# Two-stage packed attention with a gated convolution: gates per channel block, normalisation per head group, the 1e-9 as a column of the sums, v of batch 1 ahead of w_out, and a new order

## The chip, the core and the metric

The kernel runs on one core of a Trainium2 chip. A core has five engines that run beside each other, each with its own list of instructions in a fixed order: TensorE (PE, matrix products into PSUM), VectorE (DVE), ScalarE (ACT), GpSimd (POOL) and SyncE (SP), which here only issues transfers between the chip's memory and the core's SBUF. An instruction waits on semaphores for what it needs, and everything behind it on its engine waits with it.

The metric is the device time of one execution in microseconds (us). The chance of "faster" and "slower" in the prediction means a change of more than 0.5%.

## What is computed

Eight batches of eight heads, 576 rows, head size 64, and 32 packed rows per head. The packed rows attend to k and v; then q attends to the packed result, which serves as keys and as values. The heads are joined to 512 channels, which are gated by a sigmoid of a causal convolution over five rows and projected.

```python
scale = 1.0 / np.sqrt(q.shape[-1])
def sm_attn(qq, kk, vv):
    s = scale * np.matmul(qq, kk.transpose(0, 1, 3, 2))
    s = s - np.max(s, axis=-1, keepdims=True)
    a = np.exp(s)
    a = a / (np.sum(a, axis=-1, keepdims=True) + 1e-09)
    return np.matmul(a, vv)
p_packed = sm_attn(p, k, v)
out = sm_attn(q, p_packed, p_packed)
...
for k in range(K):                      # K = 5, x: the heads joined
    gate_pre += conv_w[k][None, None, :] * xp[:, k:k + S, :]
gate = 1.0 / (1.0 + np.exp(-gate_pre))
val = x @ w_val
return (gate * val @ w_out).astype(np.float32)
```

The three weight arrays arrive as 64-bit numbers and are rebuilt as 32-bit ones on the core.

## The kernel before, in words

Everything goes batch by batch. One generator function per step yields after each piece of work, and one table, `ORDER`, says which generator moves next. A token such as `g3.2` moves the gate of batch 3 by two pieces. Since every engine keeps its instructions in the order in which they are made (`InOrder`), the table is the schedule of all five engines; what waits for what follows from the data.

The steps of batch b, with the names that the trace shows:

- `load_k`, `load_q`, `load_v` ("K", "Q", "V") fetch km, qm and vm in two halves each, and `load_weights` ("L") the words of the weights. All of these go through `fetch`: a fetch waits until the fetch three before it has landed (`AT_ONCE = 3`). `load_p` ("P") fetches p for two batches outside that rule, in four small transfers, and ACT scales it. vm has two buffers, km and qm two each.
- `attn_pack` ("a"): PE makes the scores s of p and k for two groups of four heads (in PSUM). For each group g, DVE takes the maximum nb and ACT the exponential a1, with its row sums into sm. DVE adds 1e-9 to both sums and inverts them. Then for each group PE transposes a1 (at), ACT copies that to a1t, PE multiplies with vm (pv), and ACT scales the result into ppd.
- `packed_turned` ("p") transposes ppd into ppT; `packed_values` ("w") multiplies it with w_val (wp) and splits it into a rounded part wph (ACT) and a remainder wpl (DVE).
- `attn_out` ("s"): scores of q and ppT; per group DVE transposes them to t, takes the maximum mx, POOL subtracts it, and ACT takes the exponential. A column of 1e-9 stands beside each row of t.
- `weighted` ("t"): for both groups in turn, DVE sums and inverts (rs), POOL multiplies t by it, DVE transposes to a (a2 in the code), ACT rounds that to a2h, and the remainder a2l is taken by POOL (batches 0 to 2) or DVE.
- `mixed` ("x"): for batches 0 to 2 (`WHOLE`) the convolution is folded into PE: POOL multiplies ppd with the taps (kx), PE makes x out of a and kx, and ACT takes a tanh into sig. For batches 3 to 7 PE makes x, ACT copies it to xp, and `gate` ("g") computes the convolution: per block c of 128 channels ACT multiplies with the first tap, DVE adds the other four (four steps sig<-xp,cw,sig, each on the result of the one before), and ACT takes the tanh.
- `value` ("v"): per block PE multiplies a with the packed values in twelve matmuls (val), DVE joins it with the gate (sig<-sig,val, here "the last step of a gate"), ACT rounds to gvh, and POOL takes the remainder gvl.
- `project` ("o"): chunks of 128 rows; each is twelve matmuls of gvh and gvl with w_out (woh, wol). ACT copies a chunk out (osb) and SP writes it. For the last batch five chunks are begun before the last channel block is there.

The large PSUM tiles (scores, at, x, wp, val) share three buffers.

In the old order the gate of one batch is a single generator, so its blocks come strictly one after the other; the same holds for the two groups of `weighted`.

Of the kernel before, what the change touches and what calls it, by code (L numbers as in the profile page):

```python
# [57 lines left out]
v0 t1 a3.2 P4 a3 w1 O0.2 Q2 O0 v0 w1.2 v0 q2 p2 O0.2 x1 a3 x1 O0 x1 a3.2 O0 t1 a3.2 x1 L0 t1 O0.2 V3 q2 a3 x1 P4 O0.2
v1 x1 O0 K4 v1 s2 O0 V4 a3 O0 k4 a3 O0 v1 K4 O0 k4 s2 K5 s2.2 v1 s2 o0 s2 o0 p3 k4 Q3 v1.3 t2 v1.2 K5 v1 Q3 v1.2 a4 q3
o0 t2 a4.2 s2 a4.2 w2 V4 o0 s2 v1 t2 o0 w2 k5 s2 p3 a4 x2 q3 o0 v1 o0 w2 t2 s3 t2 o0 P6 Q4 t2 a4 v1 t2 s3 P6 s3 t2  # L60
s3.2 t2 s3.2 k5 s3 o0.2 a4 s3 v1 x2.3 Q4 a4 K6 a4 k5 a4.2 x2 o0 q4 t2 a4 t3 x2 v2 q4 x2 t3 a5 t3 v2 t3 a4.2 o1 t3 o0
t3 k6 K6 a5 t3 V5 v2 a5.2 t3 x3 Q5 x3 a4 v2 a5 k6 x3.2 t3 k6 v2 o1 v2 p4 v2 x3.3 t3 V5 Q5 o1 g3 a5.2 g3 p4 a5 v2 g3 o1
# [39 lines left out]
def packed_attention_gated_conv(  # L102
# [272 lines left out]
    def attn_pack(b):  # L375
# [6 lines left out]
        for g in range(G):  # L382
            nb = tile_of("nb1", [P, 1], F32, f"nb1_{b}_{g}")
            dve.tensor_reduce(nb, s1s[g], axis=AX.XY, op=ALU.max, negate=True)
            yield
# [76 lines left out]
            yield  # L462

    def weighted(b):
        rs = tile_of("rs2", [P, G, NBLK], F32, f"rs2_{b}")
        a2 = st["a2", b] = tile_of("a2", [P, G, S], F32, f"a2_{b}")
        ah = st["ah", b] = tile_of("a2h", [P, G, S], F32R, f"a2h_{b}")
        al = st["al", b] = tile_of("a2l", [P, G, S], F32R, f"a2l_{b}")
        for g in range(G):
            t3, r3 = st["t2", b][:, g], rs[:, g]  # L470
            dve.tensor_reduce(r3, t3, axis=AX.X, op=ALU.add)
            dve.reciprocal(r3, r3)
            yield
            t3 = t3[:, :, :NP]
            pool.tensor_tensor(
                t3, t3, r3.unsqueeze(2).broadcast_to([P, NBLK, NP]), op=ALU.mult
            )
            yield
            dve.transpose(a2[:, g], t3)
            yield  # L480
            act.copy(ah[:, g], a2[:, g])
            yield
            (pool if b in ON_POOL["al"] else dve).tensor_tensor(
                al[:, g], a2[:, g], ah[:, g].bitcast(F32), op=ALU.subtract
            )
            yield

# [85 lines left out]
                if c % 2:  # L573
                    yield

    def gate(b):
        if b in WHOLE:
            return
        for c in range(NC):
            x = st["xp", b, c // 2][:, c % 2]  # L580
# [3 lines left out]
            for kk in range(1, NT):
                dve.scalar_tensor_tensor(
                    acc,
                    x[:, kk : kk + S],
                    cw[:, c, kk : kk + 1],
                    acc,
                    op0=ALU.mult,  # L590
                    op1=ALU.add,
                )
                yield
            act.activation(acc, acc, AF.Tanh, scale=0.5)
            yield
# [86 lines left out]
    streams = {  # L682
        "K": load_k, "V": load_v, "Q": load_q, "P": load_p, "L": load_weights,
        "C": conv_weights, "W": value_weights, "O": out_weights,
        "k": keys, "a": attn_pack, "q": queries, "p": packed_turned, "s": attn_out, "t": weighted,
        "w": packed_values, "x": mixed, "g": gate, "v": value, "o": project,
    }
# [47 lines left out]
```

## Time and profile before

| | us |
|---|---|
| median of three runs | 284.44 (283.52 to 285.25) |
| the profiled execution | 284.7 |
| its span, first to last instruction | 282.9 |

The profile comes from one execution. Its page and the answers about its trace give, for each engine, when it was busy and what ended each idle time before an instruction: "[1.42 <-ACT sig]" means that the engine stood idle for 1.42 us and that an ACT instruction writing sig let it go on. In the rows, out<-in are the tiles written and read, then shapes, and xN the number of instructions joined in one row. Tile names leave out the numbers of batch and buffer. PEld is the loading of matmul weights, which runs beside the matmuls. SPq rows are issues of transfers; their landing comes later. Busy times of PE overlap, because matmuls are pipelined: the distance between two starts is the pace.

### The profile page before, as it was taken

The numbers are of one execution on the slowest core, as the hardware profiler recorded it, in microseconds if no ns is written. First come the engines' busy times: TensorE is split into PE (matmuls) and PEld (weight loads), VectorE is DVE, ScalarE is ACT, GpSimd is POOL, SyncE is SP. The second block draws the span as 40 slices with busy tenths as digits, with TensorE's granted clock in tenths as the row PEclk, the third lists the DMA queues.
The fourth block names the chain that finished last, engine by engine and source line by source line (L and its number), as shares of the span: only waits on it lengthen the run. The fifth ranks groups of instructions, "written<-read, shape, count | busy, mean of one in ns | idle before, by whom it ended". The sixth has DMA issues, their size and how long they took to land.

```text
span 282.9 us, 8353 instructions
## 1 busy us (share of the span) xinstructions
PE 251.4 (89%) x3603; PEld 186.8 (66%) x3603; DVE 237.2 (84%) x313; ACT 164.5 (58%) x307; POOL 129.4 (46%) x118
## 2 busy tenths in 40 slices
PE   0366397999999999999999999999999899998984
PEld 0144254776786777786878687758876688687763
DVE  2978779799789997789999999999998989687720
ACT  6245564677934664864746765667747645743321
POOL 1633577667788572423466324243156423422220
PEclk9989879999999999999999999999999999999999
DMA  7999989599649758816552540116111112111014
GB/s 258 330 292 310 226 270 264 164 238 287 179 153 306 207 161 237 257 43 203 150 180 81 191 132 37 39 75 179 66 39 41 48 63 76 39 74 39 0 50 172
DMA packets 25858, 43.54 MB, mean 154 GB/s; under 512 B 5834, under 2 KB 11998, under 8 KB 25822
## 3 DMA queue, kind: packets, MB, share of 16 engines
q1 hardware_dynamic: 25822, 43.02, 49.5%
q8 instruction: 28, 0.46, 0.7%
q14 instruction: 8, 0.07, 0.1%
HBM read 33.57 MB, written 9.44 MB: 152 GB/s over the span
## 4 chain that ended last, share of the span: by engine, by line
PE 55%; DVE 23%; ACT 9%; DMA 5%; issue 3%; POOL 2%; SPq 2%; POOLq 1%; ACTq 0%; DVEq 0%
PE o L85 20%; DVE sig L85 16%; PE val L85 11%; PE s L85 7%; PE x L85 7%; PE pv L85 4%; DMA vm<-in_v_dram 3%; ACT sig L85 3%; PE at L85 3%; PE wp L85 2%; POOL t L85 2%; SPq L85 2%; DMA p<-in_p_dram 1%; ACT gvh L85 1%; ACT osb L85 1%
## 5 line engine op out<-in xcount | busy, mean ns | idle before, releaser
L85 DVE SCALAR_TENSOR_TENSOR sig<-xp,cw,sig 128x576 f32<-128x576 f32 x80 | 75.0, 937 | 6.1 <-ACT sig L85 4.6
L85 POOL TENSOR_TENSOR gvl<-sig,gvh 128x576 fp32r<-128x576 f32 x32 | 49.3, 1541 | 55.8 <-ACT gvh L85 55.8
L85 PE MATMUL o<-woh,gvh 128*128 128x512 f32 x144 | 59.1, 411 | 0.8 <-ACT osb L85 0.7
L85 PE MATMUL o<-woh,gvl 128*128 128x512 f32 x144 | 57.2, 398 | 1.2 <-POOL gvl L85 1.1
L85 PE MATMUL o<-wol,gvh 128*128 128x512 f32 x144 | 56.9, 395 | 0.0
L85 PE MATMUL val<-a2h,wph 128*128 128x288 f32 x128 | 39.1, 305 | 0.0
L85 PE MATMUL val<-a2h,wpl 128*128 128x288 f32 x128 | 38.0, 297 | 0.9 <-DVE wpl L85 0.9
L85 PE MATMUL val<-a2l,wph 128*128 128x288 f32 x128 | 37.6, 294 | 0.0
L85 POOL TENSOR_TENSOR t<-t,rs 128x576 f32<-128x576 f32 x16 | 20.0, 1252 | 34.7 <-DVE rs L85 34.7
L85 PEld LDWEIGHTS o<-woh,gvh 128*128 128x128 f32 x144 | 27.0, 188 | 12.6 <-ACT osb L85 2.7
L85 PEld LDWEIGHTS o<-woh,gvl 128*128 128x128 f32 x144 | 27.1, 188 | 8.8 <-POOL gvl L85 2.5
L85 ACT ACTIVATE osb<-o 128x512 f32<-128x512 f32 x34 | 20.4, 599 | 18.4 <-PE o L85 14.8
L85 ACT CAST gvh<-sig 128x576 fp32r<-128x576 f32 x32 | 21.5, 671 | 16.4 <-DVE sig L85 16.0
L85 PEld LDWEIGHTS o<-wol,gvh 128*128 128x128 f32 x144 | 27.1, 188 | 5.0
L85 DVE SCALAR_TENSOR_TENSOR sig<-sig,val 128x576 f32<-128x576 f32 x32 | 23.8, 743 | 7.8 <-ACT sig L85 3.6
L85 POOL TENSOR_TENSOR t<-t,mx 128x576 f32<-128x576 f32 x16 | 21.2, 1328 | 18.3 <-DVE mx L85 18.3
L85 PEld LDWEIGHTS val<-a2h,wph 128*128 128x128 f32 x128 | 24.0, 188 | 4.4 <-issue 1.8
L85 PE MATMUL s<-kT,pT 32*32 32x288 f32 x512 | 15.5, 461 | 11.7 <-DVE kT L85 11.7
L85 PEld LDWEIGHTS val<-a2h,wpl 128*128 128x128 f32 x128 | 24.0, 188 | 2.1 <-DVE wpl L85 1.2
L85 ACT ACTIVATE sig<-sig 128x576 f32<-128x576 f32 x20 | 13.7, 685 | 19.4 <-DVE sig L85 19.1
L85 PEld LDWEIGHTS val<-a2l,wph 128*128 128x128 f32 x128 | 24.1, 188 | 0.0
L85 PEld LDWEIGHTS pv<-vm,a1t 96*32 96x32 f32 x768 | 12.8, 117 | 15.1 <-ACT p L85 5.1
(81 smaller groups left out, 444.2 us busy)
## 6 DMA issues: line engine op xcount, KB each, us to landing
km<-in_k_dram SPq DMA_DIRECT2D x16, 576.0 KB, 5.3
vm<-in_v_dram SPq DMA_DIRECT2D x16, 576.0 KB, 6.1
qm<-in_q_dram SPq DMA_DIRECT2D x16, 576.0 KB, 6.1
out_dram<-osb SPq DMA_DIRECT2D x36, 256.0 KB, 2.0
wv_words<-in_moe_w_val_dram SPq DMA_DIRECT2D x4, 512.0 KB, 4.5
wo_words<-in_moe_w_out_dram SPq DMA_DIRECT2D x4, 512.0 KB, 5.6
p<-in_p_dram SPq DMA_DIRECT2D x16, 64.0 KB, 5.9
cw_words<-in_moe_conv_w_dram SPq DMA_DIRECT2D x1, 20.0 KB
```

The source lines that it names most:

```text
L85: made = getattr(self.engine, op)(*args, **kw)
```

## The change

Five things change together.

1. The row sums of the first attention go into a new constant tile `sums`, one pair per batch and group, whose second element was set to 1e-9 by POOL at the start. DVE no longer adds 1e-9, but sums each pair into sm.
2. `weighted` is split: group 0 stays "t", group 1 becomes a stream of its own, "u". The work of each is unchanged.
3. `gate` now takes n = 4b + c and makes one block only, so that the blocks of a batch (g12 to g31) can be taken in any order.
4. The first half of v of batch 1 is fetched ahead of w_out.
5. The table is a new one over the whole length.

```diff
-V0 a0.2 W0 a1 W0 a0 W0 C0 a1 W0 a0 W0 Q0.2 a0 L0 p0 a1 K2 p0 q0.2 a1 P2 s0 a1 C0.2 s0 C0 O0 s0 O0 s0 V1 s0.2 a1 s0 O0
+V0 a0.2 W0 C0 W0 C0 a1 a0 Q0 W0 Q0 V1 a0 L0 a1 a0 K2 a1 q0.2 C0 p0 P2 p0 a1 W0 s0 a1 W0 s0 O0.2 s0.2 C0 s0.3 a1.3 O0
...
+    sums = const.tile([P, B, G, 2], F32, name="sums")
+    pool.memset(sums, 1e-9)
...
-                accum_out=sm[:, g : g + 1],
+                accum_out=sums[:, b, g, :1],
             )
             yield
-        dve.tensor_scalar_add(sm, sm, 1e-9)
+        dve.tensor_reduce(sm, sums[:, b], axis=AX.X, op=ALU.add)
...
     def weighted(b):
-        for g in range(G):
-            t3, r3 = st["t2", b][:, g], rs[:, g]
+        yield from weighted_group(b, 0)
+
+    def weighted_second(b):
+        yield from weighted_group(b, 1)
...
-    def gate(b):
-        if b in WHOLE:
-            return
-        for c in range(NC):
-            x = st["xp", b, c // 2][:, c % 2]
+    def gate(n):
+        b, c = divmod(n, NC)
+        x = st["xp", b, c // 2][:, c % 2]
```

Where the order moves instructions is best seen in the engines' own lists. First the transfers that SP issues in the front, from the first half of q of batch 0 on (vm_1_0 is the first half of v of batch 1, wo0 the first part of w_out), before and then in the changed kernel:

```order
L85 DMA qm_0_0_322<-in_q_dram 128x2x576
L85 DMA qm_0_1_324<-in_q_dram 128x2x576
L85 DMA wo0_words_327<-in_moe_w_out_dram 128x1024
L85 DMA km_2_0_335<-in_k_dram 128x2x576
L85 DMA p_2_345<-in_p_dram 32x8x64 x4
L85 DMA vm_1_0_399<-in_v_dram 96x4x384
L85 DMA vm_1_1_445<-in_v_dram 96x4x384
```
```order
L87 DMA qm_0_0_319<-in_q_dram 128x2x576
L87 DMA qm_0_1_322<-in_q_dram 128x2x576
L87 DMA vm_1_0_324<-in_v_dram 96x4x384
L87 DMA wo0_words_327<-in_moe_w_out_dram 128x1024
L87 DMA km_2_0_332<-in_k_dram 128x2x576
L87 DMA p_2_345<-in_p_dram 32x8x64 x4
L87 DMA vm_1_1_506<-in_v_dram 96x4x384
```

The first half of v has moved ahead of w_out, k and p; the second half still stands behind p.

Next ACT in the same part of the program (t2_0 is t of batch 0, a1t_1_0 and a1t_1_1 the turned exponentials of batch 1, cwb the spread taps), before and in the changed kernel:

```order
L85 ACTIVATE t2_0_350<-t2_0_350 128x18x32
L85 COPY cwb_73<-spread_429 128x5x2x64
L85 ACTIVATE t2_0_350<-t2_0_350 128x18x32
L85 COPY a1t_1_0_408<-at_1_0_409 96x768
L85 ACTIVATE p_2_345<-p_2_345 128x512
L85 CAST a2h_0_425<-a2_0_424 128x576
L85 ACTIVATE ppd_1_407<-pv_1_0_454,sm1_1_254 128x64
L85 ACTIVATE ppd_1_407<-pv_1_0_454,sm1_1_254 128x2x64
L85 COPY a1t_1_1_487<-at_1_1_488 96x768
```
```order
L87 ACTIVATE t2_0_355<-t2_0_355 128x18x32
L87 COPY a1t_1_0_409<-at_1_0_410 96x768
L87 ACTIVATE t2_0_355<-t2_0_355 128x18x32
L87 COPY cwb_73<-spread_434 128x5x2x64
L87 ACTIVATE ppd_1_408<-pv_1_0_450,sm1_1_259 128x64
L87 ACTIVATE ppd_1_408<-pv_1_0_450,sm1_1_259 128x2x64
L87 ACTIVATE p_2_345<-p_2_345 128x512
L87 COPY a1t_1_1_478<-at_1_1_479 96x768
```

The copy a1t_1_0 has moved ahead of the second exponential and of the taps, and the rounding a2h behind the second copy.

Last the end of DVE's list, from wpl of batch 7 on (sig_7_2 is block 2 of the last batch), before and in the changed kernel:

```order
L85 TENSOR_TENSOR wpl_7_3491<-wp_7_3468,wph_7_3490 128x1024
L85 SCALAR_TENSOR_TENSOR sig_7_0_3522<-xp_7_0_3419,cw_70,sig_7_0_3522 128x576 x4
L85 SCALAR_TENSOR_TENSOR sig_7_0_3522<-sig_7_0_3522,val_7_0_3508 128x576
L85 SCALAR_TENSOR_TENSOR sig_7_1_3531<-xp_7_0_3419,cw_70,sig_7_1_3531 128x576 x4
L85 SCALAR_TENSOR_TENSOR sig_7_2_3586<-xp_7_1_3421,cw_70,sig_7_2_3586 128x576
L85 SCALAR_TENSOR_TENSOR sig_7_1_3531<-sig_7_1_3531,val_7_1_3560 128x576
L85 SCALAR_TENSOR_TENSOR sig_7_2_3586<-xp_7_1_3421,cw_70,sig_7_2_3586 128x576 x3
L85 SCALAR_TENSOR_TENSOR sig_7_2_3586<-sig_7_2_3586,val_7_2_3599 128x576
```
```order
L87 SCALAR_TENSOR_TENSOR sig_7_3_3540<-xp_7_1_3423,cw_70,sig_7_3_3540 128x576
L87 SCALAR_TENSOR_TENSOR sig_7_0_3511<-sig_7_0_3511,val_7_0_3514 128x576
L87 SCALAR_TENSOR_TENSOR sig_7_2_3536<-xp_7_1_3423,cw_70,sig_7_2_3536 128x576
L87 SCALAR_TENSOR_TENSOR sig_7_1_3528<-sig_7_1_3528,val_7_1_3570 128x576
L87 SCALAR_TENSOR_TENSOR sig_7_2_3536<-xp_7_1_3423,cw_70,sig_7_2_3536 128x576
L87 SCALAR_TENSOR_TENSOR sig_7_3_3540<-xp_7_1_3423,cw_70,sig_7_3_3540 128x576
L87 SCALAR_TENSOR_TENSOR sig_7_2_3536<-sig_7_2_3536,val_7_2_3602 128x576
L87 SCALAR_TENSOR_TENSOR sig_7_3_3540<-xp_7_1_3423,cw_70,sig_7_3_3540 128x576 x2
```

The second list begins ten steps behind wpl: before, block 0 was finished right behind its four steps; now steps of other blocks stand between a chain's fourth step and its last one. On PE the last val of batch 7 has moved ahead of the first two products of the last chunks.

More of the change, by code (lines that the diff above doesn't have):

```diff
@@ L58 @@
[L58 to L62, printed above, removed]
@@ new lines @@
+V5 a5 g12 x3 s4 Q5 o1 g13 g12 a5.2 s4 v2 g12 a5 g12 s4.2 g13 o1 a5.2 s4 a5 s4 v2.2 g14 o1 g13 w3 v2.2 q5 g14 a6 o1.2
+w3 t4 Q6 a6 a5 v2 o1 a6.2 w3 g15 a5 g13 t4 s4 a5 g15 o1 q5 o1 g15 v3 p5.2 a6 g14 s4.2 o1 g15 o1 u4 g14 o1 Q6 s5 t4 v3
+o2 g14 u4 g15 v3.2 k7 s5 q6 s5 g15 v3 V6 v3 s5 o2 g14 t4 x4 o2 v3.3 u4 o2 s5.2 v3.2 s5.2 x4 v3 u4 v3 x4.2 k7 V6 o2 s5
+x4.2 a6 t4 v3.2 x4 v3 o2.2 g17 u4 a6.2 w4 a6 g16 o2 t5 u5 w4 a6 g17 a6.2 o2 g17.2 o2 a6 g18 g16 o2 g17 g19 o2 g16 w4
+a6 g16.2 g18 u5 a6 v4 u5 g18 g16 v4 t5 a6 K7 g17 g19 o3 v4.3 g18 t5 v4.2 g18 o3 g19 t5 v4 g18 q6 p6 v4 o3 g19 v4 g19
@@ L74 @@
+u7 o5.2 g27 v6 g27 x7 o5 v6 g27 u7 x7 v6 x7.2 v6.3 o5 x7 o5 t7 w7 x7 t7 w7.2 o6 g28.2 v7 o5 g29.3 g28 o6 x7 g30.2 o6
+g31 g29 g28 o6 g29 g28 g30 g31 o6 g28 o6 v7 g30 v7.2 g29 v7.4 o6 g30.2 g31 v7 o6 v7.3 g31 v7 g31.2 v7.3 o7.2 o6 o7.17
+o6.3
 """
@@ L464, in weighted, with weighted_group @@
     def weighted(b):
[L465 to L468, printed above, removed]
-        for g in range(G):
-            t3, r3 = st["t2", b][:, g], rs[:, g]
[L471 to L486, printed above, removed]
+        st["rs", b] = tile_of("rs2", [P, G, NBLK], F32, f"rs2_{b}")
+        st["a2", b] = tile_of("a2", [P, G, S], F32, f"a2_{b}")
+        st["ah", b] = tile_of("a2h", [P, G, S], F32R, f"a2h_{b}")
+        st["al", b] = tile_of("a2l", [P, G, S], F32R, f"a2l_{b}")
+        yield from weighted_group(b, 0)
+    def weighted_second(b):
+        yield from weighted_group(b, 1)
+    def weighted_group(b, g):
+        rs, a2, ah, al = (st[nm, b] for nm in ("rs", "a2", "ah", "al"))
+        t3, r3 = st["t2", b][:, g], rs[:, g]
+        dve.tensor_reduce(r3, t3, axis=AX.X, op=ALU.add)
+        dve.reciprocal(r3, r3)
+        yield
+        t3 = t3[:, :, :NP]
+        pool.tensor_tensor(
+            t3, t3, r3.unsqueeze(2).broadcast_to([P, NBLK, NP]), op=ALU.mult
+        )
+        yield
+        dve.transpose(a2[:, g], t3)
+        yield
+        act.copy(ah[:, g], a2[:, g])
+        yield
+        (pool if b in ON_POOL["al"] else dve).tensor_tensor(
+            al[:, g], a2[:, g], ah[:, g].bitcast(F32), op=ALU.subtract
+        )
+        yield
     def packed_values(b):
@@ L574, in convolved @@
                     yield
-    def gate(b):
-        if b in WHOLE:
-            return
-        for c in range(NC):
-            x = st["xp", b, c // 2][:, c % 2]
-            acc = st["sig", b, c] = tile_of("sig", [P, S], F32, f"sig_{b}_{c}")
-            act.mul(acc, x[:, :S], cw[:, c, 0:1])
-            yield
[L584 to L595, printed above, removed]
+    def gate(n):
+        b, c = divmod(n, NC)
+        x = st["xp", b, c // 2][:, c % 2]
+        acc = st["sig", b, c] = tile_of("sig", [P, S], F32, f"sig_{b}_{c}")
+        act.mul(acc, x[:, :S], cw[:, c, 0:1])
+        yield
+        for kk in range(1, NT):
+            dve.scalar_tensor_tensor(
+                acc,
+                x[:, kk : kk + S],
+                cw[:, c, kk : kk + 1],
+                acc,
+                op0=ALU.mult,
+                op1=ALU.add,
+            )
+            yield
+        act.activation(acc, acc, AF.Tanh, scale=0.5)
+        yield
     def value(b):
@@ L684, in packed_attention_gated_conv @@
         "C": conv_weights, "W": value_weights, "O": out_weights,
[L685 removed]
+        "k": keys, "a": attn_pack, "q": queries, "p": packed_turned, "s": attn_out, "t": weighted, "u": weighted_second,
         "w": packed_values, "x": mixed, "g": gate, "v": value, "o": project,
```

27 lines of the change are left out of this document (13 added, 14 removed).

## The prediction

> **What bounds the kernel now.** First the page's totals.
>
> ```profile
> span 282.9 us, 8353 instructions
> PE 251.4 (89%) x3603; PEld 186.8 (66%) x3603; DVE 237.2 (84%) x313; ACT 164.5 (58%) x307; POOL 129.4 (46%) x118
> ```
>
> PE and DVE are both near the span. Shares over the whole hide where the rest lies, so I read the busy times by stretches next.
>
> ```profile
> 0.00:50.00 50.00, 26.58 (x644) 16.22 (x658) 37.27 (x55) 26.58 (x54) 25.95 (x28) 0.90 0.96 278
> 50.00:130.00 80.00, 78.93 (x1551) 59.19 (x1520) 70.01 (x95) 50.52 (x106) 48.69 (x44) 1.00 0.68 204
> 130.00:240.00 110.00, 108.66 (x1232) 83.05 (x1230) 105.56 (x138) 70.42 (x122) 44.87 (x40) 1.00 0.30 97
> ```
>
> The columns are PE, PEld, DVE, ACT, POOL, granted clock, DMA share and GB/s. Up to 50 us the DMA engines are 96% busy and PE stands still for 23.4 us. From 50 to 240 us PE idles for 1.07 + 1.34 = 2.4 us of 190. A busy PE need not be PE at its pace, so the rows of its timeline follow, at the one place in the middle where it visibly waits.
>
> ```profile
> 222.55 0.39 PE L85 MATMUL o<-woh,gvl 128*128 128x512 f32 x1
> 222.78 0.29 PE L85 MATMUL val<-a2h,wph 128*128 128x288 f32 x1
> 223.97 0.40 PE L85 MATMUL val<-a2h,wpl 128*128 128x288 f32 x1 [0.89 <-DVE wpl L85]
> ```
>
> An output matmul takes 0.39 us from start to end, but the next instruction starts 0.23 us after it: this is the pace to measure by. 36 output chunks of 12 matmuls at 0.23 us are 99 us, the largest part of PE's work, and the change leaves every matmul in place: **PE is at its pace**. The kernel can gain only where PE waits: in the first 50 us, at this wpl, and behind the last gates. DVE is the second bound: it has 9.99 us of idle time from 50 to 130 us, but only 4.44 us from 130 to 240. The chain of waits shows what held the front:
>
> ```profile
> 25.86 9.90 DMA vm<-in_v_dram
> ...
> 40.63 0.66 PE x L85 x12
> ...
> 46.58 1.47 issue
> 48.05 1.19 PE x L85 x21
> ```
>
> PE waits for v of batch 1 from 25.86 to 35.76 us (25.86 + 9.90), and the convolution x starts at 40.63. At 46.58 lies a gap that no wait explains. PE's own timeline has the wait at its matmul:
>
> ```profile
> 35.90 1.51 PE L85 MATMUL pv<-vm,a1t 96*32 96x64 f32 x48 [4.92 <-DMA vm<-in_v_dram]
> ```
>
> **The change: v of batch 1.** The DMA queue's rows say when it can come.
>
> ```profile
> 17.12 2.16 SPq L85 DMA_DIRECT2D qm<-in_q_dram  x2
> 22.11 0.35 SPq L85 DMA_DIRECT2D wo_words<-in_moe_w_out_dram  x1
> ```
> ```profile
> DMA to landing us min/median/max: 4.4/6.1/10.2
> ```
>
> At most three fetches are under way, so the fetch behind the two of q starts when v of batch 0, three fetches earlier, has landed, at 22.11. That slot passes from w_out to the first half of v. With the median landing v is there at 28.2 us, with the longest at 32.3. Nothing is saved in bytes: w_out, k and p of batch 2 each go one place back, and so does the second half of v behind them, which stays the later of the two.
>
> The wait of 4.9 us is not won whole, because another input of the same matmul is nearly as late: a1t, which ACT copies.
>
> ```profile
> 31.60 0.68 ACT L85 ACTIVATE t<-t 128x576 f32<-128x576 f32 x1 [1.89 <-POOL t L85]
> 32.19 0.67 ACT L85 COPY cwb<-spread 128x640 f32<-128x640 f32 x1
> 33.82 0.68 ACT L85 ACTIVATE t<-t 128x576 f32<-128x576 f32 x1 [0.95 <-POOL t L85]
> 34.41 0.78 ACT L85 COPY a1t<-at 96x768 f32<-96x768 f32 x1
> ```
>
> In the old order a1t ends at 35.19, and sooner v alone would be worth 0.7 us. In the new order this copy stands directly behind the first exponential: it starts at 32.19 and ends at 32.97, so pv can start at 33.1 instead of 35.90. That is 2.8 us. The new wait is a1t behind the first t of POOL.
>
> **The normalisation per pair.** Next on PE, after a transpose, the packed values and a second pv, is the convolution of batch 0 (x at 40.63). It needs kx and both transposed halves of a2, hence POOL:
>
> ```profile
> 30.41 1.16 POOL L85 TENSOR_TENSOR t<-t,mx 128x576 f32<-128x576 f32 x1 [4.13 <-DVE mx L85]
> 32.52 1.27 POOL L85 TENSOR_TENSOR t<-t,mx 128x576 f32<-128x576 f32 x1 [0.95 <-DVE mx L85]
> 33.98 1.41 POOL L85 TENSOR_TENSOR t<-t,rs 128x576 f32<-128x576 f32 x1 [0.20 <-DVE rs L85]
> 35.34 1.55 POOL L85 TENSOR_TENSOR kx<-ppd,cwb 128x640 f32<-128x640 f32 x1
> 36.98 1.41 POOL L85 TENSOR_TENSOR a2l<-a,a2h 128x576 fp32r<-128x576 f32 x1
> 38.35 1.34 POOL L85 TENSOR_TENSOR t<-t,rs 128x576 f32<-128x576 f32 x1
> ```
>
> The split lets the second t·rs stand right behind the first, with kx after it and both a2l later. DVE's second maximum also moves ahead of the sum and its reciprocal, 0.59 + 0.17 us by the rows below. So the second subtraction starts 0.76 sooner, at 31.76, and ends at 33.0, its exponential (0.68) 33.7, the row sum and reciprocal (about 1.0, the maximum over the same tile being 0.74) 34.8, the second t·rs (1.34) 36.2 and kx (1.55) 37.8: x starts at 37.9, 2.7 us sooner. What is late next is a2l for the first val, now behind three steps of w_out on POOL: 37.8 + 3 x 1.3 + 1.41 + 1.55 + 1.41 = 46.1 us; before it lie x, which now runs until 49.24 (48.05 + 1.19), and the scores of batch 2, so it is hidden as long as these come no more than 3 us sooner. ACT's product on p of batch 2 also stands ahead of the second a1t copy. I take 2.7 us, or 4.2 if the unexplained 1.47 us do not return, and between them **3.3**. The bounds are 0.7 (v alone) and 6.4 (the whole wait of 4.9 and the gap).
>
> **The 1e-9 as a column.** The addition becomes a sum over two elements.
>
> ```profile
> L85 DVE TENSOR_REDUCE mx<-t 128x18 f32<-128x576 f32 x16 | 11.9, 744 | 0.3
> L85 DVE TENSOR_SCALAR sm<-sm 128x2 f32<-128x2 f32 x8 | 4.7, 591 | 0.2 <-ACT a L85 0.2
> L85 DVE RECIPROCAL sm<-sm 128x2 f32<-128x2 f32 x8 | 1.3, 166 | 0.3
> ```
>
> The trace has no sum of this size. It lies between the reciprocal of the same tile (8 x 0.166 = 1.3 us) and the big sums (8 x 0.744 = 6.0): DVE gains 3.4 or loses 1.3. Two elements are nearest to the reciprocal, so 3.4 us less DVE work, of which I count 2.2 behind the front (five or six of the eight). PE is the bound, so I book nothing for it; it is cover.
>
> That row's mean of 591 for two elements is more than three times the reciprocal's 166. [...]
>
> **The gates per channel block, and the order.** No instruction is added; the same 20 chains of six operations interleave. The gain is at the end, where DVE waits for the tanh of the chain it has just finished, and PE for gvl:
>
> ```profile
> 257.16 0.82 DVE L85 SCALAR_TENSOR_TENSOR sig<-xp,cw,sig 128x576 f32<-128x576 f32 x1 [1.42 <-ACT sig L85]
> ...
> 262.86 0.76 DVE L85 SCALAR_TENSOR_TENSOR sig<-sig,val 128x576 f32<-128x576 f32 x1 [0.75 <-ACT sig L85]
> ```
> ```profile
> 260.39 0.39 PE L85 MATMUL o<-wol,gvh 128*128 128x512 f32 x1
> 261.55 0.50 PE L85 MATMUL o<-woh,gvl 128*128 128x512 f32 x1 [0.77 <-POOL gvl L85]
> ```
>
> Of the last batch's chains DVE loses 1.42 and 0.75 us here; in the new order other chains' steps stand in both places, so some 2.2 us go. PE loses 1.16 - 0.23 = 0.93 us at 261.55; the new order also puts its last val, twelve matmuls, ahead of these products, which covers that. At 223.97 PE lost 0.89 us to wpl, ahead of which DVE now has the same work less the shorter sums. Together **1.8 us**, bounds 0 (DVE comes no sooner than PE) and 1.8. Against them I set **0.7 us** of new waits: the middle has 2.4 us of PE idle time now, and a new order has others (bounds 0 and 2.4).
>
> Sum: 284.7 us (span 282.9 and 1.8 around it) - 3.3 - 1.8 + 0.7 = 280.3. The profiled run is 0.3 us over the median of 284.44; for the median that gives **280.0 us**, 1.6% less.
>
> **The rivals.** *Nothing is carried.* PE starts sooner, but DVE, which idles for only 4.4 us from 130 to 240, comes no sooner to the gates. Then the front's gain is waited away at val and o, and only the wpl wait and part of the end stay: 284.4 - 1 = 283.4. For it speaks DVE's 96% there; against it that its work ahead of each gate is not more, that PE outputs come sooner, and that 10 us of idle time lie before 130.
>
> *The loads come too late.* w_out, k and p of batch 2 land later, and ACT waits for p ahead of the a1t of batch 1. p is issued just ahead of 25.86 now and one fetch later then, about 2.2 us (the two of q took 2.16); by the longest landing above it is there at 28.1 + 10.2 = 38.3. The product, the copy (0.78 each at most) and the second pv then leave x at 40.6, where it is now: the same 283.4.
>
> *Slower: the interleaved gates meet POOL.* The price is in the group's row:
>
> ```profile
> L85 DVE SCALAR_TENSOR_TENSOR sig<-xp,cw,sig 128x576 f32<-128x576 f32 x80 | 75.0, 937 | 6.1 <-ACT sig L85 4.6
> 246.33 3.38 DVE L85 SCALAR_TENSOR_TENSOR sig<-xp,cw,sig 128x576 f32<-128x576 f32 x4 [0.19 <-ACT sig L85]
> 251.13 4.61 DVE L85 SCALAR_TENSOR_TENSOR sig<-xp,cw,sig 128x576 f32<-128x576 f32 x4
> 252.84 1.44 POOL L85 TENSOR_TENSOR gvl<-sig,gvh 128x576 fp32r<-128x576 f32 x1 [7.86 <-ACT gvh L85]
> ```
>
> A clean step takes 0.82 us (the end of one overlaps the next: 3.38 for four), so 80 would take 65.6; 9.4 us are lost. The chain at 251.13 is 1.2 us longer than the one at 246.33, and POOL works beside it. From 130 to 240 POOL is busy 41% of the time. If the interleaving doubles these losses, DVE has 9.4 us more; 1.1 us of its idle time is left after the front's gain, and 2.2 us come off with the sums: 280.0 + 6.1 = 286.1, and more if more steps meet. It is slower than before from 4.4 + 1.1 + 2.2 = 7.7 us more, six or seven such steps. [...]
>
> *More than forecast.* The gap at 46.58 goes and every gvl wait too: 284.4 - 4.2 - 1.8 = 278.4 without new waits, and 276.2 with the whole wait of 4.9 us besides the gap.
>
> **How the numbers follow.** My forecast 0.55, more than forecast 0.2, nothing carried or loads late 0.14, slower 0.11. The range leaves out a tenth on either side: 276.0 (front wait, gap and end all gone) to 286.0 (the gates' losses doubled). A measurement of this kernel tells 0.5%, 1.4 us, from no change: faster 0.75, same 0.14, slower 0.11.
>
> **What would show it.** In the changed profile: v of batch 1 issued near 22 us and landed by 29; its pv at about 33 after an ACT wait, x at about 38, the first k scores of batch 2 at 45 to 47 instead of after 49.2; sm sums near 0.17 us each; no ACT wait over 1 us on DVE after 240; the sig<-xp group at 75 us or less; PE without gaps from 50 us. I am wrong if p or the second v holds ACT or PE before 40 us, if PE shows new waits for DVE or POOL from 60 to 240 us, or if the sig group has grown.

## The result, and the profile after

| | before | changed |
|---|---|---|
| median, us | 284.44 (283.52 to 285.25) | 279.74 (279.26 to 280.44) |
| the profiled execution, us | 284.7 | 279.26 |
| its span, us | 282.9 | 277.5 |

The ratio of the times is 0.985 (95% interval 0.981 to 0.989). The forecast was 280.0. The time was right; where it came from was not, as the rows below show. First the totals of the changed kernel and its busy times by stretches (PE, PEld, DVE, ACT, POOL, granted clock, DMA share, GB/s):

```profile
span 277.5 us, 8356 instructions
PE 252.7 (91%) x3603; PEld 187.6 (68%) x3603; DVE 227.8 (82%) x313; ACT 164.1 (59%) x307; POOL 132.0 (48%) x119
```
```profile
0.00:50.00 50.00, 30.74 (x689) 17.77 (x689) 36.65 (x55) 27.43 (x56) 25.70 (x28) 0.90 0.93 279
50.00:130.00 80.00, 78.98 (x1518) 59.38 (x1500) 68.86 (x99) 51.06 (x105) 49.76 (x44) 1.00 0.70 203
130.00:240.00 110.00, 110.00 (x1245) 83.85 (x1243) 102.70 (x137) 70.64 (x125) 50.05 (x44) 1.00 0.31 98
```

PE has no idle time left from 130 to 240 us, and DVE has lost 9.4 us of work over the whole. The grouped rows of DVE say where: the gate steps (75.0 us before) and the sums (4.7 us before, as additions). In the rows stand busy time, mean of one in ns, and idle time before them.

```profile
L87 DVE SCALAR_TENSOR_TENSOR sig<-xp,cw,sig 128x576 f32<-128x576 f32 x80 | 66.1, 870 | 1.5 <-ACT sig L87 1.2
...
L87 DVE TENSOR_REDUCE sm<-sums 128x2 f32<-128x4 f32 x8 | 1.1, 142 | 0.2 <-ACT a L87 0.2
```

To see which stage gave the time, take two points on PE that have the same set of matmuls ahead of them in both kernels, whatever their order (689 and 3275): the first val, and the packed values wp of batch 6. PE's timeline, first of the kernel before, then of the changed one:

```profile
51.23 0.40 PE L85 MATMUL val<-a2h,wph 128*128 128x288 f32 x1
...
218.87 1.09 PE L85 MATMUL wp<-wv,ppT 64*32 64x512 f32 x16
```
```profile
50.26 0.40 PE L87 MATMUL val<-a2h,wph 128*128 128x288 f32 x1
...
217.17 1.09 PE L87 MATMUL wp<-wv,ppT 64*32 64x512 f32 x16
```

Up to the first val the changed kernel gains 51.23 - 50.26 = 0.97 us. From there to wp it takes 166.91 us instead of 167.64, 0.73 less. From wp to the end of the span it takes 60.31 instead of 64.06: **3.75 us of the 5.4 come from the last 64 us**. The prediction had put 3.3 into the front and 1.8 behind wp.

These two points and the end are the measure for all experiments below. The ratios compare fast executions, but the profiled one of f2 was a slow one (284.5 us), so of its three stretches only the last is used.

### The profile page after: what moved, and what is told of

It reads as the page before. It is cut to its first block, busy times and chain, and to the rows that moved or that the text cites. A ratio compares the mean times of both kernels' runs of the same rounds, so it can differ in the third digit from the quotient of the medians.

```text
span 277.5 us, 8356 instructions
## 1 busy us (share of the span) xinstructions
PE 252.7 (91%) x3603; PEld 187.6 (68%) x3603; DVE 227.8 (82%) x313; ACT 164.1 (59%) x307; POOL 132.0 (48%) x119
## 4 chain that ended last, share of the span: by engine, by line
PE 85%; DMA 8%; DVE 2%; ACT 1%; SPq 1%; issue 1%; POOL 0%; ACTq 0%
PE o L87 37%; PE val L87 19%; PE x L87 8%; PE s L87 8%; PE pv L87 5%; DMA km<-in_k_dram 4%; PE at L87 4%; PE wp L87 3%; DMA qm<-in_q_dram 3%; DMA wv_words<-in_moe_w_val_dram 2%; PE ppTt L87 1%; SPq L87 1%; DVE mx L87 1%; DVE t L87 1%; DVE qT L87 1%
## 5 line engine op out<-in xcount | busy, mean ns | idle before, releaser
L87 POOL TENSOR_TENSOR gvl<-sig,gvh 128x576 fp32r<-128x576 f32 x32 | 51.0, 1595 | 69.5 <-ACT gvh L87 69.4
L87 DVE SCALAR_TENSOR_TENSOR sig<-xp,cw,sig 128x576 f32<-128x576 f32 x80 | 66.1, 870 | 1.5 <-ACT sig L87 1.2
L87 PE MATMUL val<-a2h,wpl 128*128 128x288 f32 x128 | 37.9, 296 | 0.5 <-issue 0.5
L87 PE MATMUL s<-kT,pT 32*32 32x288 f32 x512 | 16.9, 479 | 11.9 <-DVE kT L87 11.6
L87 POOL TENSOR_TENSOR t<-t,rs 128x576 f32<-128x576 f32 x16 | 20.6, 1296 | 8.6 <-DVE rs L87 7.1
L87 PEld LDWEIGHTS pv<-vm,a1t 96*32 96x32 f32 x768 | 13.7, 123 | 13.4 <-issue 3.7
L87 DVE STREAM_TRANSPOSE qT<-qm 128x1152 f32<-128x1152 f32 x16 | 21.6, 1357 | 0.8 <-DMA qm<-in_q_dram 0.8
```

Source lines behind the costliest of these rows:

```text
L87: made = getattr(self.engine, op)(*args, **kw)
```

## The experiments

Times are medians. "To val", "to wp" and "to end" are the three stretches in us, from each run's profiled execution. The ratio is to runs of the kernel before on the same chip.

| run | time | ratio (95%) | to val | to wp | to end |
|---|---|---|---|---|---|
| before | 284.44 | 1 | 51.23 | 167.64 | 64.06 |
| changed | 279.74 | 0.985 (0.981-0.989) | 50.26 | 166.91 | 60.31 |
| e1_cw_sooner | 280.56 | 0.990 (0.986-0.993) | 51.71 | 166.83 | 60.32 |
| e2_cw_wo | 280.33 | 0.988 (0.983-0.992) | 49.77 | 166.78 | 60.32 |
| e3_v_late | 279.94 | 0.985 (0.981-0.990) | 50.09 | 166.51 | 60.32 |
| e4_before_v_sooner | 284.51 | 1.004 (1.001-1.006) | 50.22 | 167.79 | 64.07 |
| e5_before_sums | 284.55 | 1.002 (1.000-1.005) | 52.69 | 166.56 | 64.10 |
| e6_after_scalar | 282.26 | 0.995 (0.992-0.998) | 50.08 | 168.75 | 60.91 |
| e7_last_serial | 284.64 | 1.003 (1.000-1.006) | 48.77 | 167.85 | 65.14 |
| e8_all_serial | 314.75 | 1.108 (1.104-1.113) | 51.25 | 189.75 | 71.42 |
| f1_front_of_after | 285.77 | 1.005 (1.002-1.008) | 52.39 | 169.15 | 64.06 |
| f2_tail_of_before | 283.08 | 0.994 (0.991-0.998) | 51.08 | 168.95 | 62.69 |
| f3_busy_pe | 280.42 | 0.988 (0.984-0.992) | 50.38 | 168.96 | 60.34 |
| f4_busy_pe_cw_wo | 280.29 | 0.986 (0.981-0.990) | 51.64 | 166.37 | 60.33 |

The last column repeats to 0.1 us wherever the order behind wp is the same (e6 apart, of which more below). The first varies by 3.6 us between changed, e7 and f1 (50.26, 48.77, 52.39), whose order on PE is the same up to there: a single front says little. The medians say more: they lie 4.70 us apart, 3.75 of that is behind wp, and so less than 1 us is left for everything ahead of it.

### What held the front: the copy of cw

The forecast had the first pv of batch 1 at 33.1 us, behind its a1t copy. It starts at 36.06, 1.5 us after that copy has ended. PE and DVE of the changed kernel:

```profile
36.06 1.51 PE L87 MATMUL pv<-vm,a1t 96*32 96x64 f32 x48 [3.17 <-ACT cwb L87]
```
```profile
33.61 1.34 DVE L87 TENSOR_SCALAR wo_words<-wo_words 128x512 uint32<-128x512 uint32 x1
...
35.84 0.12 DVE L87 COPY cw<-cwps 128x20 f32<-128x20 f32 x1
```

The row names ACT's cwb, with which pv shares nothing. But pv goes into the PSUM tile "mid", of which there is one, and cwps sits in it until DVE has copied cw, at 35.96.

```diff
-s0 O0.2 s0.2 C0 s0.3 a1.3 O0 s0 t0 C0 s0 C0 | C0 u0 t0
+s0 O0.2 s0.2 C0 s0.3 C0 a1.3 O0 s0 t0 s0 C0 | C0 u0 t0        # e1
+s0 O0.2 s0.2 C0 s0.3 C0 a1.3 s0 t0 s0 C0 | C0 u0 O0 t0        # e2
```

e1_cw_sooner:

> The changed kernel, with DVE's copy of the transposed taps (cw<-cwps) 5 places sooner on DVE, behind the first maximum instead of behind the first row sum. Theory 1: the first pv of batch 1 waits at 36.06 us because cwps holds the only PSUM buffer called mid until that copy ends at 35.96. Then pv starts behind its own a1t copy, at 34.6 to 34.8, x some 1.1 to 1.4 us sooner than 41.64 (kx, which ends at 40.48, is next), and the time is 278.4 to 279.0 us. Rival: pv waits for ACT's cwb, as its row names it. Then pv stays at 36.0 and the time at 279.7.

e2_cw_wo:

> As the run before, and in addition the first word step of w_out on DVE (1.34 us at 33.61) behind the two row sums instead of ahead of them. Theory 1: the row sums start at 34.0 instead of 34.87, both t times rs and kx come 1 us sooner, x is held only by PE's own chain from pv (34.7 + 5.6 = 40.3 us), and the time is 278.2 to 278.6. Rival (cwb): 279.3 to 279.7, since pv stays at 36.0 and x with it.

PE of e1 and of e2:

```profile
35.48 1.51 PE L87 MATMUL pv<-vm,a1t 96*32 96x64 f32 x48 [0.79 <-ACT a1t L87]
```
```profile
34.20 1.51 PE L87 MATMUL pv<-vm,a1t 96*32 96x64 f32 x48 [1.85 <-ACT a1t L87]
```

In both runs pv now starts 0.05 us after a1t has ended (35.43 and 34.15 on ACT) and names it: the theory of the PSUM tile holds, and the releaser printed in the changed kernel was wrong. But neither run is faster. In e2 pv is 1.86 us sooner and x 1.85 (39.79 instead of 41.64), but only twelve of its products are done before 41.72; the first val is 0.5 us sooner, and the median is not below 279.74. In the profile of e1 the granted clock stayed at 0.50 from 28.1 to 45.1 us, and the first 80 products of x took 4.49 us instead of 2.78, which hides the sooner pv there. So a sooner pv of batch 1 does not by itself bring the front's end sooner.

### Sooner v by itself

e3_v_late puts the first half of v back behind p of batch 2 in the changed order; e4_before_v_sooner does this one edit in the old order.

```diff
-Q0 W0 Q0 V1 a0 L0 a1 a0 K2 a1 q0.2 C0 p0 P2 p0
+Q0 W0 Q0 a0 L0 a1 a0 K2 a1 q0.2 C0 p0 P2 V1 p0                # e3
-Q0.2 a0 L0 p0 ... O0 s0 V1 s0.2
+Q0.2 V1 a0 L0 p0 ... O0 s0 s0.2                               # e4
```

> The changed kernel with the first half of v of batch 1 fetched where it was before, behind p of batch 2. If the sooner fetch is what the front gained by, pv of batch 1 starts at 38 or later (v lands one fetch later than in the old order) and the time is 281 or more. If the copy of cw holds that pv anyway, v lands at about 35.8, pv stays near 36, the second half of q comes 0.8 to 1 us sooner than now (qT at 25.7 instead of 26.65), and the time is within 0.5 us of 279.7.

> The kernel before with one edit: the first half of v of batch 1 fetched directly behind q of batch 0. By the prediction: pv starts behind its a1t copy at 35.2 instead of 35.90 and the time is 0.7 us less, 283.7. Rival: v takes its share of the DMA engines from the second half of q, qT comes 1 us later and all behind it, pv is then at 36 or later, and the time is 284.4 to 285.4.

DVE of the changed kernel, then of e3:

```profile
26.65 1.38 DVE L87 STREAM_TRANSPOSE qT<-qm 128x1152 f32<-128x1152 f32 x1 [0.84 <-DMA qm<-in_q_dram]
```
```profile
24.82 2.63 DVE L87 STREAM_TRANSPOSE qT<-qm 128x1152 f32<-128x1152 f32 x2
```

With v under way beside it, the second half of q lands later, and DVE waits 0.84 us for it; with v late both transposes run through. The time of e3 is that of the changed kernel: v lands late, and pv starts at 35.65, still behind cw. In the old order the sooner v costs 0.1 to 0.6% instead of gaining 0.7 us. PE and DVE of e4:

```profile
35.65 1.51 PE L85 MATMUL pv<-vm,a1t 96*32 96x64 f32 x48 [4.26 <-ACT a1t L85]
```
```profile
26.27 1.38 DVE L85 STREAM_TRANSPOSE qT<-qm 128x1152 f32<-128x1152 f32 x1 [0.42 <-DMA qm<-in_q_dram]
```

PE's wait for v has turned into one for a1t, and pv starts 0.25 us sooner. The rival has the median on its side, and the rows fit it in kind: the second transpose of q ends at 27.65 instead of 27.04. That q pays for v is not shown beyond that; the profiled execution itself reaches the first val at 50.22, sooner than before, without the stop of 1.47 us.

### The whole front by itself

f1_front_of_after takes the changed order up to the last piece of t0 (some 47 us) and then everything that is left in the old order.

> The changed kernel's order up to the last step of batch 0's normalisation (near 47 us), and from there all that is left in the old order (gates one after the other, the two halves of the normalisation one after the other). By the prediction the front is worth 3.3 us: the time is 280.5 to 281.5 (kernel before: 283.9). By the traces, in which the first val starts at 50.26 instead of 51.23, it is worth about 1 us: 282.5 to 283.5.

Measured: 285.77, 0.2 to 0.8% slower than before. No 3.3 us, and not even 1. In its profiled execution the first val starts at 52.39, and the part behind wp takes 64.06, as in the kernel before. Why the old rest is slower behind the new front, and not equal, is open. In this one execution PE stopped for 1.63 us ahead of 73.03, and its clock was 0.50 from 74.1 to 77.5; whether the other executions have such stops is not known.

### The column of the sums

e5_before_sums makes this edit alone, the tile `sums` with it; e6_after_scalar undoes it in the changed kernel, so that it has no such tile.

```diff
-    sums = const.tile([P, B, G, 2], F32, name="sums")
-    pool.memset(sums, 1e-9)
...
-        dve.tensor_reduce(sm, sums[:, b], axis=AX.X, op=ALU.add)
+        dve.tensor_scalar_add(sm, sm, 1e-9)                   # e6
```

> The kernel before with one edit: 1e-9 as a column of the sums, a sum over two elements in place of the tensor_scalar. By the prediction DVE does 3.4 us less (each sum about 0.15 us instead of 0.59) and the time stays within 0.5 us of the kernel before, since PE is the bound and DVE's work is cover. Rival: PE's waits in the middle are waits for DVE, as the 0.89 us for wpl at 223.97 is; then that wait shortens or goes and the time falls by 1 us or more.

> The changed kernel with the tensor_scalar again in place of the column and its sum. By the prediction DVE does some 3.4 us more and the time stays within 0.5 us of the changed kernel's 279.7. Rival: DVE is close enough to being the bound that the time rises by 1 us or more, with waits of PE for DVE from 60 to 240 us or for wpl near 222.

In the old order the time does not fall, as forecast. In the new order the column is worth about 2.5 us (282.26 against 279.74; the intervals do not touch). Two things make it up. The first is a stretched addition. DVE, ACT and PE of e6, and DVE of the changed kernel at the same place:

```profile
65.81 1.41 DVE L87 TENSOR_SCALAR sm<-sm 128x2 f32<-128x2 f32 x1
```
```profile
69.94 0.62 ACT L87 CAST woh<-wo_top 128x512 fp32r<-128x512 f32 x1 [1.62 <-DVE wo_top L87]
```
```profile
71.56 0.88 PE L87 MATMUL pv<-vm,a1t 96*32 96x64 f32 x48 [0.78 <-ACT ppT L87]
```
```profile
65.70 0.15 DVE L87 TENSOR_REDUCE sm<-sums 128x2 f32<-128x4 f32 x1
```

One addition on two elements takes 1.41 us. DVE's steps on w_out come later by that, and one of them takes 1.17 us there instead of 0.39; ACT waits 1.62 us for their result, the copy of ppT stands behind it on ACT, and PE waits 0.78 us. The eight additions of e6 took 0.13 to 1.41 us, the eight sums of the changed kernel 0.11 to 0.16. What goes with a long addition can be seen in the kernel before, where the eight take 0.16 to 1.57 us. The longest one and POOL beside it, and POOL of the changed kernel at the sum of 65.70:

```profile
91.38 1.57 DVE L85 TENSOR_SCALAR sm<-sm 128x2 f32<-128x2 f32 x1
```
```profile
91.25 1.58 POOL L85 TENSOR_TENSOR kx<-ppd,cwb 128x640 f32<-128x640 f32 x1
```
```profile
65.17 1.43 POOL L87 TENSOR_TENSOR a2l<-a,a2h 128x576 fp32r<-128x576 f32 x1 [0.61 <-ACT a2h L87]
```

Five additions of the kernel before start while a POOL instruction runs: they take 0.46 to 1.57 us and end 0.02 to 0.12 us after it. The three that start with POOL idle take 0.16. Of the eight sums of the changed kernel five run beside POOL, and none of them takes more than 0.16.

The second is larger, and the prediction does not have it: PE's own pace. Here are the first and the last of 48 output products that follow each other without a wait, in the changed kernel and in e6:

```profile
255.75 0.39 PE L87 MATMUL o<-woh,gvh 128*128 128x512 f32 x1
...
266.50 0.40 PE L87 MATMUL o<-woh,gvl 128*128 128x512 f32 x1
```
```profile
257.76 0.39 PE L87 MATMUL o<-woh,gvh 128*128 128x512 f32 x1
...
268.72 0.39 PE L87 MATMUL o<-woh,gvl 128*128 128x512 f32 x1
```

The 47 steps take 10.75 us with the column and 10.96 without. It is so in all profiles: the mean step between two such products is 0.2331 us in the three kernels without the tile `sums` (before, e4, e6) and 0.2293 to 0.2296 in the eleven that have it, in either order. Added up over the output products of e6 this is 1.3 of the 2.2 us by which its span is longer, 0.60 of them behind wp. In the old order it shows too: e4 and e5 have no stop of PE behind the first val, and from there to wp e5 takes 166.56 us instead of 167.79. That the medians do not follow there is not explained. The tile takes 128 bytes of each partition (8 batches x 2 groups x 2 x 4), and gvh and gvl are allocated behind it in the program. Whether this sets the pace, or something else in the edit, no run tells.

### The end

Ahead of val of batch 6 DVE makes wpl. Before, then changed:

```profile
217.57 5.21 DVE L85 SCALAR_TENSOR_TENSOR sig<-xp,cw,sig 128x576 f32<-128x576 f32 x4
222.70 1.21 DVE L85 TENSOR_TENSOR wpl<-wp,wph 128x1024 fp32r<-128x1024 f32 x1
```
```profile
219.42 1.23 DVE L87 TENSOR_TENSOR wpl<-wp,wph 128x1024 fp32r<-128x1024 f32 x1 [0.50 <-ACT wph L87]
```

The old order has four stretched gate steps ahead of wpl (5.21 us; four clean ones take 3.38). In the new one DVE is there before wph is. That took PE's wait away. For the last batch, the waits of weight loads (total us, times, longest) from 240 to 283 us, before and changed:

```profile
PEld o L85 <- POOL gvl L85: 2.5, 3, 1.2
PEld o L85 <- ACT osb L85: 1.4, 2, 1.0
...
PEld o L85 <- DVE osb L85: 0.5, 1, 0.5
```
```profile
PEld o L87 <- ACT osb L87: 1.1, 1, 1.1
PEld o L87 <- ACT a2h L87: 0.8, 1, 0.8
PEld o L87 <- DVE osb L87: 0.5, 1, 0.5
```

Three waits for gvl are gone; the others come to about as much as before. f2_tail_of_before tells the two apart: the changed order up to the first gate step of the last batch (some 242 us), then all that is left in the old order.

> The changed kernel's order up to the first gate step of the last batch (near 242 us), and from there what is left in the old order (that batch's gate chains one after the other, val behind the products as before). By the prediction only the 0.93 us of PE's wait for gvl come back: 280.5 to 281.0. By the traces PE loses 2.4 us more behind 225 us in the old order (1.2 to the last val, 1.2 in the last products): 281.8 to 282.6. If the last batch's order were worth all of the 4.9 us that the run with serial chains lost, the time is 284 or more.

It took 283.08 us, and 62.69 from wp to the end: the last batch's order is worth 62.69 - 60.31 = 2.38 us, at the same pace of PE, since both have the tile `sums`. The rest is 64.06 - 62.69 = 1.37; of it 1.06 arises at the val of the kernel before that waits for wpl (223.97). The last step of the gates on DVE and the last gvl on POOL, in the changed kernel and in f2:

```profile
260.45 0.76 DVE L87 SCALAR_TENSOR_TENSOR sig<-sig,val 128x576 f32<-128x576 f32 x1 [0.75 <-ACT sig L87]
```
```profile
262.06 1.43 POOL L87 TENSOR_TENSOR gvl<-sig,gvh 128x576 fp32r<-128x576 f32 x1 [2.98 <-ACT gvh L87]
```
```profile
268.55 0.75 DVE L86 SCALAR_TENSOR_TENSOR sig<-sig,val 128x576 f32<-128x576 f32 x1 [0.75 <-ACT sig L86]
```
```profile
270.15 1.43 POOL L86 TENSOR_TENSOR gvl<-sig,gvh 128x576 fp32r<-128x576 f32 x1 [3.83 <-ACT gvh L86]
```

The last gvl ends 14.0 us ahead of the span's end in the changed kernel (277.5 - 263.5) and 11.1 in f2. From the first product that needs the last gvl to the end it takes 11 us in both, the last 4 of them copying and writing. So f2 waits for this gvl, while the new order has 3 us to spare and is bound by PE and, for 0.69 us, by a copy of a finished chunk. That fits the last column: in the old order the pace of PE does not show there (64.06 without the tile, 64.10 with it), in the new one it does (60.91 and 60.31).

e7_last_serial and e8_all_serial keep the changed order's places for gate steps but fill them one chain after the other: for the last batch, and for all five.

```diff
-g28.2 v7 o5 g29.3 g28 o6 x7 g30.2 o6 g31 g29 g28 ...
+g28.2 v7 o5 g28.3 g28 o6 x7 g29.2 o6 g29 g29 g29 ...          # e7
```

> The changed kernel with the four gate chains of the last batch one after the other, in the same places of the order (24 steps, first all of block 0, then of 1, 2, 3). Theory of the prediction: the interleaving is what takes DVE's waits for ACT's tanh away; serial, DVE loses 1.4 and 0.75 us again near 257 and 262, the last gates and gvl come 1 to 2 us later and the time is 280.7 to 282. Rival: PE no longer waits at the end because its last val stand ahead of the output products, whatever the gates do; then the time stays within 0.5 us of 279.7.

> The changed kernel with the gate chains of all five batches (3 to 7) one after the other in the same places of the order. Theory: the interleaving gave DVE its 9 us (waits for ACT's first product, and a step that starts while the last one of another chain still ends); serial, the group sig<-xp goes back from 66 us to 74 or more, PE waits again for wpl and gvl, and the time is 282 to 284. Rival: DVE's 9 us are off PE's path but for the last batch; then the time is that of the run with the last batch alone serial.

e7 loses 4.9 us, more than either theory, and its first val was even sooner. DVE of e7:

```profile
248.67 3.38 DVE L86 SCALAR_TENSOR_TENSOR sig<-xp,cw,sig 128x576 f32<-128x576 f32 x4 [2.44 <-ACT sig L86]
253.47 2.53 DVE L86 SCALAR_TENSOR_TENSOR sig<-xp,cw,sig 128x576 f32<-128x576 f32 x3 [1.42 <-ACT sig L86]
...
259.53 2.26 DVE L86 SCALAR_TENSOR_TENSOR sig<-xp,cw,sig 128x576 f32<-128x576 f32 x2 [1.48 <-ACT sig L86]
```

DVE waits for ACT's first product ahead of each chain, because that product stands behind the chain before. So interleaving is what takes these waits away, but e7 overstates it: the old order, also serial, places ACT's products better and loses only 2.38 us. PE of e7 also waits 2.38 us for a copy of a chunk ahead of 247.49, and its clock is 0.50 from 248.1 to 251.5, which f2 does not have. e8 shows the same in the extreme (DVE waits 24.2 us ahead of the gate steps, and the time is 314.75, far outside both expectations). It says nothing on the old order, and nothing follows from it but that these places only suit interleaved chains.

### Is it the clock?

In the changed kernel PE's granted clock is 0.50 from 35.1 to 42.0 us, in the last 0.9 us of an idle time of 3.17 us and behind it. f3_busy_pe and f4_busy_pe_cw_wo fill PE's idle time in the front with matmuls that nobody reads.

```diff
+    warm = one("warm", "out")[:, :P]
+    def keep_busy(n):
+        while True:
+            pe.matmul(warm, ident, ident, start=True, stop=True)
+            yield
...
-p0 P2 p0 ... s0 a1 W0 s0 ... t0 C0 s0 C0 |
+Z0.2 p0 P2 p0 ... Z0.2 s0 a1 W0 s0 ... t0 C0 s0 C0 Z0.12 |     # f3
```

> The changed kernel with 16 matmuls of the identity with itself (128x128, their result is read by nobody) on PE where it waits in the front: 2 ahead of the first transposes of packed values, 2 ahead of the scores of batch 0, 12 behind the spread of the taps, ahead of the pv that starts at 36.06. They change no output. Theory: the granted clock of 0.50 from 36 to 42 us follows from PE's idle time ahead of it; kept busy, it is granted 1.00 there, pv takes 0.88 instead of 1.51 us and the packed values 1.0 instead of 1.96, x starts at about 40.5 (kx is next), and the time is 1 us less, 278.7, with less spread between runs. Rival: the clock there depends on something else, or DVE and POOL hold x anyway; then the time stays at 279.7 or rises by what the 16 matmuls delay.

> The run before with 12 of the matmuls (2, 2 and 8), and the copy of cw and the first word step of w_out moved as in the earlier run with both. Theory: with cw out of the way pv follows its a1t at 34.2, with the full clock x starts at about 38.5 instead of 39.8, and the time is 1 to 2 us under the changed kernel's: 277.7 to 278.7. Rival: what is won before 50 us is waited away for DVE's step on w_out and ACT behind it near 70 us; then the time stays at 279.5 to 280.3.

Windows of the changed kernel and of f3 (columns as above), and pv in f3:

```profile
36.00:40.00 4.00, 3.94 (x76) 2.21 (x76) 3.97 (x7) 2.29 (x5) 3.93 (x3) 0.50 0.96 324
```
```profile
36.00:40.00 4.00, 3.30 (x106) 2.10 (x107) 3.96 (x9) 2.54 (x6) 3.64 (x3) 1.00 0.89 248
```
```profile
36.35 0.88 PE L87 MATMUL pv<-vm,a1t 96*32 96x64 f32 x48 [0.40 <-ACT cwb L87]
```

The clock is 1.00 instead of 0.50, and pv takes 0.88 instead of 1.51 us: with PE kept busy, the clock did not fall there. How long a stop it takes is not settled. In the changed kernel the stretch at 0.50 begins 2.2 us into the 3.17 of idle time, and in f1 and f2 the clock fell to 0.50 for 3.4 us behind a stop of 1.63 us. Behind the 2.69 us of e5 (last section) it did not fall.

But the time does not drop, and the first val stays at 50.38. Two rows of x in f3:

```profile
40.83 2.67 PE L87 MATMUL x<-a,kx 32*64 32x288 f32 x80 [0.31 <-POOL kx L87]
...
45.92 2.17 PE L87 MATMUL x<-a,kx 32*64 32x288 f32 x56 [0.40 <-issue]
```

x starts at 40.83 instead of 41.64, now held by kx on POOL, and what was won is lost again around a stop of PE ahead of 45.92, for which the profile names no releaser (last section). So this one profile does not say what the full clock is worth; the median shows no gain. POOL sets a further limit, the changed kernel first, then f3:

```profile
36.07 2.72 POOL L87 TENSOR_TENSOR t<-t,rs 128x576 f32<-128x576 f32 x2 [1.40 <-ACT cwb L87]
38.75 1.73 POOL L87 TENSOR_TENSOR kx<-ppd,cwb 128x640 f32<-128x640 f32 x1
...
47.36 1.59 POOL L87 TENSOR_TENSOR a2l<-a,a2h 128x576 fp32r<-128x576 f32 x1
```
```profile
47.42 1.85 POOL L87 TENSOR_TENSOR a2l<-a,a2h 128x576 fp32r<-128x576 f32 x1
```

From the two t·rs to the second a2l POOL works almost without a pause for 12.9 us, and it starts 0.14 us behind rs on DVE (35.93; the cwb that the row names is no input of it). The sixth product of the first val needs this a2l and cannot come sooner than 48.95 in the changed kernel or 49.27 in f3, whose clock was 1.00 all the way from 24 to 52 us. It starts at 51.03 in the changed kernel, so the limit is near but was not reached. In f4 pv moves up once more, and PE runs into the next input:

```profile
39.48 0.88 PE L87 MATMUL pv<-vm,a1t 96*32 96x64 f32 x48 [1.38 <-DMA vm<-in_v_dram]
```

That is the second half of v, which the sooner first half does not bring sooner. The clock then fell to 0.50 from 41.7 to 45.1 in f4, and the 48 products of x from 41.53 on took 3.08 us. No median lies below that of the changed kernel.

## Why the prediction was right in its time and wrong in its parts

- **The front, 3.3 us: failed.** pv of batch 1, forecast at 33.1, started at 36.06 (35.90 before), and x, forecast at 37.9, at 41.64 (40.63 before). The step that failed is "so pv can start at 33.1", in two ways. a1t itself was late: its copy was put at 32.19 to 32.97 and ran from 33.81 to 34.59, because DVE came to the first maximum at 31.20 instead of 29.58, and its wait of 0.84 us for q is a part of that. And a1t was named as the only late input: the PSUM tile held by cwps until DVE's copy was missed, though the order now puts that copy behind a step of w_out. The next step failed with it: the second row sum was put at 33.7 to 34.8, but both sums stand behind the same step of w_out on DVE and run from 34.87. "Sooner v alone would be worth 0.7" fell as well: e4 shows a loss. The 0.97 us by which the first val came sooner is not this mechanism's: the profile before has the stop of 1.47 us ahead of it, and the changed one has no such stop there.
- **"What is late next is a2l", and hidden: right.** It was put at 46.1 and ended at 48.95, but val came behind PE's own x and scores and did not wait for it.
- **"The change leaves every matmul in place: PE is at its pace": failed.** The matmuls stayed, the pace did not: 0.2331 us per output product became 0.2294, which is 1.6 us over 432 of them (an estimate). The sum has no term for that.
- **The end, 1.8 us: the mechanism was right, the size was not.** It is 3.75. The wpl wait was booked at 0.89 and is worth 1.06 to 1.37; of three waits for gvl only the one at 261.55 was priced (0.93), and the last batch is worth 2.38. The bound "0 to 1.8" was too narrow, because I summed visible idle times instead of the distance between two points.
- **New waits, 0.7: did not come** behind the front. From first val to wp the changed kernel takes 0.73 us less, but between equal orders this stretch varies by over 2 us (e7, f3 and f4: 167.85, 168.96, 166.37), so its sign is not settled. The pace alone would give 1.0 there (264 output products, an estimate).
- **The sums as cover: right for the old order (e5), wrong for the new one (e6)**, where one stretched addition lies on PE's path. The size was right: 0.142 us each, 0.17 foreseen.
- **The rivals.** "Nothing is carried" had the front's result right, though not its reason (nothing was won there that could be waited away), and missed the end. Late loads: ACT did not wait for p, but q was late. The slower case, gates that meet POOL more often, did not occur: the sig<-xp step fell from 937 to 870 ns.

Too much by 2.3 in the front, too little by 1.9 at the end and by 1.4 in between (0.7 us of waits that didn't come, 0.73 gained): the errors nearly cancelled, 5.4 us between the profiled executions against 4.4 forecast. That the time came out right is luck. Of the 4.70 us between the medians the end is shown; what is left ahead of wp is about what the pace alone would give, and no run shows a gain of the new order there.

## What to carry to other kernels

To price a change of order, find points with the same work ahead of them and compare the distances between these; single waits miss the loads and the small ones beside them. When one input comes sooner, list all that the instruction waits for, the buffer it writes to included, and follow the next engine's chain to its end before booking the gain. Compare the pace of equal instructions as well: an edit that adds a small tile changed it here (0.2331 us per output product without it, 0.2293 to 0.2296 with it), and it looked like a gain of the order. An operation that is cover in one order can be the bound in the next, so an edit that only saves work off the path may decide whether another edit pays.

## What was not expected of the hardware

**PE stops behind the same counts of matmuls.** The gap of 1.47 us that the prediction could not explain has relatives. PE of the kernel before, of e5 and of f1:

```profile
48.05 1.19 PE L85 MATMUL x<-a,kx 32*64 32x288 f32 x21 [1.47 <-issue]
```
```profile
49.51 1.19 PE L85 MATMUL x<-a,kx 32*64 32x288 f32 x21 [2.69 <-issue]
```
```profile
73.03 0.75 PE L86 MATMUL pv<-vm,a1t 96*32 96x64 f32 x35 [1.63 <-issue]
```

The trace's transfer records have a queue for instructions with 28 packets of 16 KB in an execution. Set beside such gaps:

| run | PE resumes at | behind matmul no. | gap | a packet ended |
|---|---|---|---|---|
| before | 24.68 | 221 | 0.87 | 1.54 us sooner |
| before | 48.05 | 601 | 1.47 | 1.47 |
| before | 71.27 | 1109 | 0.75 | 1.47 |
| changed | 64.46 | 983 | 0.47 | 1.33 |
| changed | 70.73 | 1110 | 0.55 | 1.41 |
| e5 | 49.51 | 601 | 2.69 | 1.63 |
| f1 | 25.16 | 221 | 1.18 | 1.62 |
| f1 | 73.03 | 1109 | 1.63 | 1.49 |
| f2 | 66.43 | 983 | 1.63 | 1.53 |
| f3 | 57.73 | 855 | 0.97 | 1.45 |

Over all executions such gaps fall only behind matmuls 221, 474, 601, 727, 855, 983 and 1109 or 1110 (as the records count them): 126 to 128 apart, or twice that. With their weight loads that is about 256 instructions, and over the whole 3603 matmuls and 3603 loads are 257 per packet. In the rows of the table PE goes on 1.3 to 1.6 us after a packet has ended. In f3 the added matmuls (32 records) lie ahead, so that other work stands at these places, and the gaps still come behind 601, 727 and 855: the count places them, not the work. All lie in the first 75 us, where the DMA engines are busiest (0.93 up to 50 us in the rows above, 0.31 behind 130). They add up to 0 to 4.1 us per execution (3.1 in the profile of before, 1.0 in that of the changed kernel, none in e1 and e4, 4.1 in f3), so they are part of the scatter of the first two stretches. That PE waits for its own instructions there fits these records, but no run changed the packets, so it is not shown.

**Interleaved gate steps on DVE start 0.1 us sooner than serial ones.** In e7 four serial gate steps take 3.38 us and three 2.53, 0.85 a step; in the changed kernel eleven interleaved ones run in one row:

```profile
243.41 8.23 DVE L87 SCALAR_TENSOR_TENSOR sig<-xp,cw,sig 128x576 f32<-128x576 f32 x11
```

That is 0.75 a step. The prediction's 0.82 for a clean step is the step's length; the pace of serial ones is 0.85. The group's busy time fell by 8.9 us, from 75.0 to 66.1. Not all of it comes from sooner starts: the mean step also got shorter, from 937 to 870 ns, which is 5.4 us over 80 steps. Seven of them take more than 0.9 us, twelve before. Some 3.5 us are left for the sooner starts.
